# One decode step, attention beside a gated MLP: `w_out` as five rows on 128 lanes and seven rows on 32 lanes, all on SyncE's queue

## The chip, the cores and the metric

The kernel runs on one core of a Trainium2 chip. The metric is the device time of one execution in microseconds (us), from launch to the output in memory; smaller is better. Three runs of the kernel before took 662.22, 662.36 and 663.16 us, so the median is 662.36.

## The reference

For four tokens (batch 4, one position each, D = 640) the kernel adds a residual, an attention branch over a long cache and a gated MLP. Cut to what matters:

```python
xn = layernorm(x)                                   # x: 4 x 1 x 640, bf16
# A: 32 heads of 128, a cache of 4096 positions per head and batch element
q = (xn @ wq).reshape(4, 1, 32, 128).transpose(0, 2, 1, 3)
p = softmax(einsum('bhqd,bhkd->bhqk', q, k_cache) * 128 ** -0.5)
A = einsum('bhqk,bhkd->bhqd', p, v_cache).transpose(0, 2, 1, 3).reshape(4, 1, 4096) @ wo
# B: w_in 640 x 1728, w_out 864 x 640, Fh = 864
z = gelu(einsum('bsd,df->bsf', xn, w_in))
z1, z2 = z[..., :Fh], layernorm(z[..., Fh:])
g = einsum('ts,bsf->btf', w_sp, z2) + b_sp[None, :, None]
B = einsum('bsf,fd->bsd', z1 * g, w_out)
out = x + A + B
```

Each of the two caches is 134.2 MB; `w_out` is 1.1 MB of 282.2 MB read in all.

## The kernel before

**Attention.** The work is cut into 16 units, one for each group of eight heads and batch element (`NU` = 16). A unit's keys are 8.4 MB, held as 128 partitions by four pieces of 16 KB. The ring `k_ring` has seven places for such pieces; the values of a unit fill the one buffer `v_all`. For each piece, DVE multiplies keys by the query row (L514, 4.4 us), folds the halves (L520, 2.3 us), PE sums over the remaining 64 columns with an identity (L529), and DVE reduces (L542). PE then weighs the values (L599).

**Order of the loads.** All large loads are issued by SyncE (SP) on one DMA queue, in the order of the list `loads`. `pump()` issues the next entry as soon as the program has passed the last use of its places; the instruction itself then waits on semaphores. The list starts with half of unit 0's keys, then `load_w`, then the other half, then unit 1's keys. The first load of all, `wq`, is issued ahead of the list. `wq` and `w_in` lie in `v_all`, so the first values can be loaded only when the gated MLP has read its weights (the load at L157). Unit 2's keys wait for the first piece of unit 1 (the load at L146 that starts at 76.58 us).

**The gated MLP.** `gmlp()` is a generator whose steps are laid between the first key pieces. It multiplies `w_in` by the normalised tokens (L380, into `zT`), goes through GELU and the layer norm in a chain of small DVE steps (L390 to L474) with two PE matmuls of its own (L409, L456), and multiplies by `w_out` (L480), adding to `out_ps`.

**How `w_out` lies.** Its 864 rows are 6 x 128 + 96. The first 768 rows stand as six rows per partition: five of them (6,400 bytes a partition) in `v_all`, loaded at L120, and the sixth (1,280 bytes a partition) in `p_m`, loaded at L121. `p_m` is the buffer of the masked weights, which is not written before unit 0's softmax ends. The last 96 rows stand as four rows on each of 24 partitions, also in `p_m`, loaded by ScalarE's (ACT's) queue in five transfers of 5, 5, 5, 5 and 4 lanes (L115); a transfer takes every fifth lane. That makes `NFC` = 10 terms, six of 128 lanes and four of 24.

**The end.** The last values come in pieces, then `wo` for the last head group in six transfers (L210, L213); PE multiplies, ACT copies, and the result goes out in two transfers.

Of the kernel before, what the change touches and what calls it, by code (L numbers as in the profile page):

```python
# [10 lines left out]
BF16 = mybir.dt.bfloat16  # L11
ACT = mybir.ActivationFunctionType
ALU = mybir.AluOpType
# [4 lines left out]
def kernel(  # L18
# [14 lines left out]
    nc = tc.nc  # L33
    P = nc.NUM_PARTITIONS
    Bsz, Sq, D = A_x.shape
# [3 lines left out]
    Fh = F // 2  # L39
# [7 lines left out]
    QD = 32  # L47
    NQ = P // QD
    HT = 8
# [9 lines left out]
    RW = 8  # L59
    QW = HC * Dh  # L60
    RING = 2 * NK - 1
    NFF = Fh // P
    FR = 4
    FT = (Fh - NFF * P) // FR
    NFC = NFF + FR
    LS = 5
    NOH = D // 2
    CB = 4
    NG = NR // CB
# [8 lines left out]
    const = ctx.enter_context(tc.tile_pool(name="const", bufs=1))  # L78
    work = ctx.enter_context(tc.tile_pool(name="work", bufs=1))
    small = ctx.enter_context(tc.tile_pool(name="small", bufs=2))  # L80
    once = ctx.enter_context(tc.tile_pool(name="once", bufs=1))
    PSUM = bass.MemoryType.PSUM
    ps_s = ctx.enter_context(tc.tile_pool(name="ps_s", bufs=2, space=PSUM))
    ps_pv = ctx.enter_context(tc.tile_pool(name="ps_pv", bufs=2, space=PSUM))
# [3 lines left out]

    pad.tile([P, 96], FP32, name="pad")

    p_m = const.tile([P, 2, NG, CB, HT], BF16, name="p_m")
    x_bf = const.tile([Bsz, D], BF16)
    nc.scalar.dma_start(out=x_bf[:], in_=A_x.flatten_outer_dims())

# [6 lines left out]
    w_in_sb = v_all[:, DC * HD : DC * (HD + F)].rearrange("p (c n) -> p c n", c=DC)  # L101


    NV = NFF - 1
    at_v = -(-DC * (HD + F) // 256) * 256
    w_out_sb = v_all[:, at_v : at_v + NV * D].rearrange("p (k n) -> p k n", k=NV)
    p_w = p_m[:].rearrange("p n g c h -> p (n g c h)")
    at_p = -(-D // 256) * 256
    w_row_sb = p_w[:, 0:D]
    w_end_sb = p_w[:, at_p : at_p + FR * D].rearrange("p (r n) -> p r n", r=FR)  # L110
    nc.sync.dma_start(out=wq_sb, in_=A_wq.rearrange("(p c) n -> p c n", c=DC))

    w_end_rows = B_w_out[NFF * P : Fh].rearrange("(p r) n -> p r n", r=FR)
    for l in range(LS):
        nc.scalar.dma_start(out=w_end_sb[l:FT:LS], in_=w_end_rows[l:FT:LS])  # L115

    def load_w():
        nc.sync.dma_start(out=w_in_sb, in_=B_w_in.rearrange("(p c) n -> p c n", c=DC))
        w_rows = B_w_out[0 : NFF * P].rearrange("(p k) n -> p k n", k=NFF)
        nc.sync.dma_start(out=w_out_sb, in_=w_rows[:, 0:NV])  # L120
        nc.sync.dma_start(out=w_row_sb, in_=w_rows[:, NV])  # L121

    def run_of(cache, u):
        hg, b = divmod(u, Bsz)
# [49 lines left out]
    def wo_load(hg):  # L174
        return (lambda: load_wo(hg)), [WO_AT]

    loads = [k_load(0, 0, 2), (load_w, []), k_load(0, 2, 4), k_load(1)]
    for u in range(NU - 4):
        loads += [v_load(u), k_load(u + 2)]
        if u % Bsz == Bsz - 1:  # L180
# [188 lines left out]
    gm["ac"] = work.tile([1, 2 * Bsz], FP32, name="ac")  # L369
    gm["yT"] = work.tile([P, NFC, Bsz], BF16, name="yT")  # L370

    def gmlp():
        zz, gw, gt, gz = (gm[n] for n in ("zz", "gw", "gt", "gz"))
        zT = ps_pv.tile([P, 2, NFC, Bsz], FP32, tag="pv", name="zT")
        for t in range(2):
            f1 = t * Fh + NFF * P
            w_t = w_in_sb[:, :, t * Fh : f1].rearrange("p c (f k) -> p c k f", k=NFF)
            for k in range(NFC):
                for c in range(DC):
                    nc.tensor.matmul(  # L380
                        out=zT[: P if k < NFF else FT, t, k, :],
                        lhsT=w_t[:, c, k, :]
                        if k < NFF
                        else w_in_sb[:, c, f1 + k - NFF : f1 + FT * FR : FR],
                        rhs=xnT[:, c, 0:Bsz],
                        start=(c == 0),
                        stop=(c == DC - 1),
                    )
        yield
        nc.vector.tensor_copy(out=zz[:, :, 0:NFF, :], in_=zT[:, :, 0:NFF, :])  # L390
        nc.vector.tensor_copy(out=zz[:FT, :, NFF:], in_=zT[:FT, :, NFF:])
        nc.vector.tensor_tensor(out=gw[:], in0=zz[:], in1=zz[:], op=ALU.mult)
        nc.vector.tensor_scalar(
            out=gw[:], in0=gw[:], scalar1=0.044715, scalar2=1.0, op0=ALU.mult, op1=ALU.add
        )
        nc.vector.tensor_tensor(out=gw[:], in0=gw[:], in1=zz[:], op=ALU.mult)
        nc.scalar.activation(
            out=gt[:], in_=gw[:], func=ACT.Tanh, scale=math.sqrt(2.0 / math.pi)
        )
        yield  # L400
        nc.vector.tensor_scalar(
            out=gt[:], in0=gt[:], scalar1=1.0, scalar2=0.5, op0=ALU.add, op1=ALU.mult
        )
        nc.vector.tensor_tensor(out=gz[:, 0:2], in0=zz[:], in1=gt[:], op=ALU.mult)
        sq = gz[:, 2, :, :]
        nc.vector.tensor_tensor(out=sq, in0=gz[:, 1, :, :], in1=gz[:, 1, :, :], op=ALU.mult)

        s_ps = ps_m.tile([1, 2, NFC, Bsz], FP32, tag="m", name="ln_ps")
        nc.tensor.matmul(  # L409
            out=s_ps[:], lhsT=ones_sq[:, 0:1], rhs=gz[:, 1:3], start=True, stop=True  # L410
        )
        yield
        st, ac = gm["st"], gm["ac"]
        mean_t = st[:, 0:Bsz]
        ex2_t = st[:, Bsz : 2 * Bsz]
        var_t = st[:, 2 * Bsz : 3 * Bsz]
        rst_t = st[:, 3 * Bsz : 4 * Bsz]
        tmp_t = st[:, 4 * Bsz : 5 * Bsz]
        nc.vector.tensor_reduce(
            out=st[:, 0 : 2 * Bsz].rearrange("o (s b) -> o s b", s=2),  # L420
            in_=s_ps[:].rearrange("o s k b -> o s b k"),
            axis=AX.X,
            op=ALU.add,
        )
        nc.vector.tensor_scalar(
            out=st[:, 0 : 2 * Bsz],
            in0=st[:, 0 : 2 * Bsz],
            scalar1=1.0 / float(Fh),
            scalar2=None,
            op0=ALU.mult,  # L430
        )
        nc.vector.tensor_tensor(out=tmp_t, in0=mean_t, in1=mean_t, op=ALU.mult)
        nc.vector.tensor_tensor(out=var_t, in0=ex2_t, in1=tmp_t, op=ALU.subtract)
        nc.scalar.activation(
            out=rst_t, in_=var_t, func=ACT.Sqrt, bias=eps_tile[:1], scale=1.0
        )
        wsp_t = work.tile([1, 1], FP32, name="wsp_t")
        nc.vector.tensor_copy(out=wsp_t[:], in_=wsp_bf[:])
        bsp_t = work.tile([1, 1], FP32, name="bsp_t")
        nc.vector.tensor_copy(out=bsp_t[:], in_=bsp_bf[:])  # L440
        yield
        nc.vector.reciprocal(out=rst_t, in_=rst_t)
        nc.vector.tensor_scalar(
            out=ac[:, 0:Bsz], in0=rst_t, scalar1=wsp_t[:, 0:1], scalar2=None, op0=ALU.mult
        )
        nc.vector.tensor_tensor(out=tmp_t, in0=ac[:, 0:Bsz], in1=mean_t, op=ALU.mult)
        nc.vector.tensor_scalar(
            out=ac[:, Bsz : 2 * Bsz],
            in0=tmp_t,
            scalar1=-1.0,  # L450
            scalar2=bsp_t[:, 0:1],
            op0=ALU.mult,
            op1=ALU.add,
        )
        ac_ps = ps_m.tile([P, 2 * Bsz], FP32, tag="m", name="ac_ps")
        nc.tensor.matmul(  # L456
            out=ac_ps[:], lhsT=ones_sq[0:1, :], rhs=ac[:], start=True, stop=True
        )
        ac_sb = work.tile([P, 2 * Bsz], FP32, name="ac_sb")
        nc.scalar.copy(out=ac_sb[:], in_=ac_ps[:])  # L460
        yield
        nc.vector.tensor_tensor(
            out=sq,
            in0=gz[:, 1, :, :],
            in1=ac_sb[:, None, 0:Bsz].to_broadcast([P, NFC, Bsz]),
            op=ALU.mult,
        )
        nc.vector.tensor_tensor(
            out=sq,
            in0=sq,  # L470
            in1=ac_sb[:, None, Bsz : 2 * Bsz].to_broadcast([P, NFC, Bsz]),
            op=ALU.add,
        )
        nc.vector.tensor_tensor(out=gm["yT"][:], in0=gz[:, 0, :, :], in1=sq, op=ALU.mult)  # L474
        w_terms = [w_out_sb[:, k] for k in range(NV)] + [w_row_sb]
        w_terms += [w_end_sb[:FT, r] for r in range(FR)]
        for k in range(NFC):
            w = P if k < NFF else FT
            for half in range(2):
                nc.tensor.matmul(  # L480
                    out=out_sum(half),
                    lhsT=gm["yT"][:w, k, :],
                    rhs=w_terms[k][:, half * NOH : (half + 1) * NOH],
                    start=False,
                    stop=False,
                )
        yield
# [150 lines left out]
    def group_turn(hg):  # L638
# [2 lines left out]


        o_q = gr.pop(hg)[:].rearrange("p (q j) -> p q j", j=JR)
        o_n = once.tile([P, JR, PAR, QH], BF16, name="o_n")
        for e in range(PAR):
            nc.vector.scalar_tensor_tensor(  # L646
                out=o_n[:, :, e, :].rearrange("p j q -> p q j"),
# [3 lines left out]
                op0=ALU.mult,  # L651
                op1=ALU.mult,
            )
        o_t = once.tile([P, JR, QD], BF16, name="o_t")
        nc.vector.transpose(
            out=o_t[:].rearrange("p j q -> p (j q)"),
            in_=o_n[:].rearrange("p j e q -> p (j e q)"),
        )
        o_s = once.tile([P, JR, Bsz], BF16, name="o_s")
        nc.vector.tensor_tensor(  # L660
            out=o_s[:], in0=o_t[:, :, 0:Bsz], in1=o_t[:, :, Bsz : 2 * Bsz], op=ALU.add
        )
        gr[hg] = [o_s[:, j, :] for j in range(JR)]

# [160 lines left out]
```

## Time and profile before

| | us |
|---|---|
| median of three runs | 662.36 |
| runs | 662.22 to 663.16 |
| span of the profiled execution, first to last instruction | 660.5 |
| median less that span | 1.9 |
| DVE busy | 524.9 (79%) |
| PE busy | 310.9 (47%) |
| ACT busy | 29.8 (5%) |
| read from memory | 282.24 MB, 427 GB/s over the span |

Of the profiled execution only the span is recorded, no device time of its own. The page gives each engine's busy time, 40 slices of the span with the busy share of each engine in tenths, the DMA queues, and a chain of waits followed back from the last instruction. A time in the trace counts from the start of the span. The trace also holds the start and length of each DMA packet; q1 is SP's queue, q10 is ACT's, q8 and q14 carry instructions.

### The profile page before, as it was taken

The page shows a single profiled execution, that of the slowest core. Times are in us where ns is not written, and L with a number is a line of the kernel's source. Part 1 is how long each engine was busy: PE and PEld are TensorE (multiplying, and loading weights), DVE is VectorE, ACT ScalarE, POOL GpSimd, SP SyncE. Part 2 cuts the span into 40 slices and gives each one's busy share as a digit, 9 for nine tenths or more (in the row PEclk, how much of TensorE's full clock was granted, in tenths as well). Part 3 has the DMA queues.
Part 4 walks back from the last instruction along what each step waited for, and adds up shares of the span by engine and source line. Part 5 has one row for each costly group of instructions (what it writes and reads, how often), then busy time and mean ns, then how long its engine had stood idle before and what let it go on. Part 6 is the DMA issues. An engine that isn't in the chain of part 4 may idle for free.

```text
span 660.5 us, 4704 instructions
## 1 busy us (share of the span) xinstructions
PE 310.9 (47%) x2035; PEld 135.7 (21%) x2035; DVE 524.9 (79%) x332; ACT 29.8 (5%) x73; POOL 2.7 (0%) x12
## 2 busy tenths in 40 slices
PE   0274363526527362472536336362462633736366
PEld 0131122212203121130212112121130221212124
DVE  2578988959598795969959598695969969999950
ACT  0020000000000000000000000000000000000000
POOL 1000000000000000000000000000000000000000
PEclk9756686766768677576767768677576767678765
DMA  9999999999999999999999999999999999999997
GB/s 372 435 448 429 430 441 437 438 425 437 430 433 438 433 433 438 433 434 425 437 437 438 421 433 438 441 438 433 429 426 441 430 433 445 411 428 437 457 400 281
DMA packets 8113, 282.56 MB, mean 428 GB/s; under 512 B 888, under 2 KB 2180, under 8 KB 2588
## 3 DMA queue, kind: packets, MB, share of 16 engines
q1 hardware_dynamic: 8024, 282.12, 99.0%
q8 instruction: 16, 0.26, 0.1%
q10 hardware_dynamic: 68, 0.13, 0.1%
q14 instruction: 5, 0.04, 0.0%
HBM read 282.24 MB, written 0.01 MB: 427 GB/s over the span
## 4 chain that ended last, share of the span: by engine, by line
DMA 60%; DVE 30%; PE 9%; issue 1%; ACT 0%; DVEq 0%; SPq 0%
DMA k_ring<-in_A_k_cache_dram 52%; DVE k_ring L514 15%; DVE k_ring L520 8%; PE s_ps L529 7%; DMA v_all<-in_A_v_cache_dram 4%; DMA k_ring<-in_A_wo_dram 3%; DVE s_sb L542 2%; DVE p_m L575 1%; DVE m L551 1%; PE out_ps L668 1%; DVE o_n L646 1%; PE zT L380 1%; PE pv L599 1%; DVE mt L553 0%; PE out_ps L480 0%
## 5 line engine op out<-in xcount | busy, mean ns | idle before, releaser
L514 DVE TENSOR_TENSOR k_ring<-k_ring,qbc 128x8192 bf16<-128x8192 bf16 x64 | 282.7, 4418 | 86.3 <-DMA k_ring<-in_A_k_cache_dram 86.3
L529 PE MATMUL s_ps<-k_ring,ident 128*128 128x512 bf16 x512 | 201.1, 564 | 313.7 <-DVE k_ring L520 313.5
L529 PEld LDWEIGHTS <-ident 128*128 128x128 bf16 x512 | 65.4, 129 | 427.7 <-issue 383.7
L520 DVE TENSOR_TENSOR k_ring<-k_ring 128x4096 bf16<-128x4096 bf16 x64 | 145.9, 2279 | 0.0
L599 PE MATMUL pv<-v_all,p_m 128*32 128x512 bf16 x960 | 60.2, 407 | 0.0
L542 DVE TENSOR_REDUCE s_sb<-s_ps 128x64 f32<-128x512 f32 x64 | 43.6, 682 | 5.7 <-PE s_ps L529 5.7
L575 DVE TENSOR_TENSOR p_m<-p_c,own 128x2048 bf16<-128x2048 bf16 x16 | 36.5, 2284 | 0.7 <-ACT p_c L564 0.7
L599 PEld LDWEIGHTS <-p_m 128*32 128x32 bf16 x992 | 25.8, 103 | 39.4 <-issue 17.1
L564 ACT ACTIVATE p_c<-s_sb,nm 128x256 bf16<-128x256 f32 x16 | 8.1, 508 | 331.2 <-DVE nm L558 331.2
L630 PEld LDWEIGHTS o_ps<-o_rows,pick 128*128 128x128 f32 x96 | 19.5, 280 | 4.1 <-issue 3.0
L630 PE MATMUL o_ps<-o_rows,pick 128*128 128x128 f32 x96 | 18.6, 357 | 0.0
L611 ACT COPY o_rows<-pv 128x512 f32<-128x512 f32 x16 | 9.4, 586 | 167.4 <-PE pv L599 167.4
L293 DVE TENSOR_SCALAR q_rows<-q_ps 128x512 bf16<-128x512 f32 x2 | 1.4, 692 | 12.3 <-PE q_ps L285 12.3
L786 DVE TENSOR_TENSOR o_n_last<-o_last,rden_all 128x32 bf16<-128x32 f32 x1 | 0.2, 192 | 12.3 <-PE o_last L778 12.3
L504 ACT CAST qbc<-qbc_ps 128x128 bf16<-128x128 f32 x16 | 4.3, 266 | 101.7 <-PE qbc_ps L496 101.7
L285 PE MATMUL q_ps<-v_all,xnT 128*32 128x512 bf16 x40 | 4.3, 618 | 8.9 <-DMA v_all<-in_A_wq_dram 8.9
L551 DVE TENSOR_REDUCE m<-s_sb 128x1 f32<-128x256 f32 x16 | 6.7, 420 | 0.6
L496 PE MATMUL qbc_ps<-q_rows,of_row 128*128 128x128 bf16 x32 | 6.0, 277 | 0.6 <-DVE q_rows L293 0.6
L496 PEld LDWEIGHTS <-of_row 128*128 128x128 bf16 x32 | 4.2, 134 | 8.3 <-issue 7.8
L668 PE MATMUL out_ps<-k_ring,o_s 128*4 128x320 bf16 x48 | 4.4, 331 | 2.2 <-DVE o_s L660 2.2
L685 PE MATMUL o_last<-hot,o_rows 128*128 128x8 f32 x32 | 4.9, 280 | 0.7 <-ACT o_rows L611 0.7
L685 PEld LDWEIGHTS o_last<-hot,o_rows 128*128 128x128 f32 x32 | 4.8, 225 | 1.8 <-ACT o_rows L611 1.6
(89 smaller groups left out, 74.6 us busy)
## 6 DMA issues: line engine op xcount, KB each, us to landing
k_ring<-in_A_k_cache_dram SPq DMA_DIRECT2D x6, 4096.0 KB, 24.8
v_all<-in_A_v_cache_dram SPq DMA_DIRECT2D x2, 4096.0 KB, 28.8
v_all<-in_A_wq_dram SPq DMA_DIRECT2D x1, 5120.0 KB
k_ring<-in_A_v_cache_dram SPq DMA_DIRECT2D x1, 4096.0 KB
k_ring<-in_A_wo_dram SPq DMA_DIRECT2D x3, 1280.0 KB, 20.1
v_all<-in_B_w_in_dram SPq DMA_DIRECT2D x1, 2160.0 KB
k_ring<-in_A_v_cache_dram SPq DMA_DIRECT2D x1, 2048.0 KB
k_ring<-in_A_v_cache_dram SPq DMA_DIRECT2D x1, 1024.0 KB
```

Source lines behind the costliest of these rows:

```text
L496: nc.tensor.matmul(out=qb_ps[:], lhsT=of_row[:, e, b].rearrange("p k f l -> p (k f l)"), rhs=q_rows[e][:, hg, :], start=(e == 0), stop=(e ...
L514: nc.vector.tensor_tensor(out=t, in0=t, in1=qbcs[u][:, None, :].to_broadcast([P, HC, Dh]), op=ALU.mult)
L520: nc.vector.tensor_tensor(out=t[:, :, 0:HD2], in0=t[:, :, 0:HD2], in1=t[:, :, HD2:Dh], op=ALU.add)
L529: nc.tensor.matmul(out=s[:], lhsT=ident[:], rhs=t[:, :, g * RW : (g + 1) * RW], start=(g == 0), stop=(g == m - 1),)
L542: nc.vector.tensor_reduce(out=scores[u][:, r * HC : (r + 1) * HC], in_=sums_ps.pop(n)[:], axis=AX.X, op=ALU.add,)
L551: nc.vector.tensor_reduce(out=m1[:], in_=scores[u][:], axis=AX.X, op=ALU.max)
L575: nc.vector.tensor_tensor(out=p_m[:, u % 2], in0=p_c.pop(u)[:].rearrange("p (g c) -> p g c", c=CB)[:, :, :, None].to_broadcast([P, NG, CB, HT]
L599: nc.tensor.matmul(out=pvs[u][cg * QD : (cg + 1) * QD, :], lhsT=p_m[:, u % 2, g0 + n].rearrange("p c h -> p (c h)"), rhs=v_at[:, n * CB : ...
L611: nc.scalar.copy(out=o[:].rearrange("p c d -> p (c d)"), in_=pvs.pop(u)[:])
L630: nc.tensor.matmul(out=gr[hg][:], lhsT=pick[:, c, Bsz - 1 - b : P + Bsz - 1 - b], rhs=o[:, c, :], start=(b == 0 and c == 0), stop=(b == Bs ...
L668: nc.tensor.matmul(out=out_sum(half), lhsT=o, rhs=wo_sb[:, n, half * NOH : (half + 1) * NOH], start=False, stop=(hg == HG - 1 and n == HT ...
L685: nc.tensor.matmul(out=o_last[0][:, :, :, u % Bsz], lhsT=o[:, c, :], rhs=hot[:, c, :].rearrange("p (k e) -> p k e", e=PAR), start=(c == 0) ...
```

## The change

`w_out` is laid out anew. The first 640 rows stand as five rows per partition in `v_all` (one transfer, 6,400 bytes a partition). The other 224 rows stand as seven rows on each of 32 partitions, in the buffer that `p_m` occupies, loaded by four transfers of eight lanes (8,960 bytes a lane, every fourth lane). These four are issued by SP, behind the first half of unit 0's keys and ahead of `w_in`. ACT issues none of `w_out`. The terms number 12 instead of 10: five of 128 lanes and seven of 32. The buffer grows so that the seven rows fit (4,480 elements), and the small tiles `o_n`, `o_t` and `o_s` of `group_turn` move from a pool of their own into its end.

```diff
-    NFF = Fh // P
-    FR = 4
-    FT = (Fh - NFF * P) // FR
-    NFC = NFF + FR
-    LS = 5
+    FA, FL, LS = 5, 32, 4
+    FB = (Fh - FA * P) // FL
+    NFC = FA + FB
...
-    p_m = const.tile([P, 2, NG, CB, HT], BF16, name="p_m")
+    p_buf = const.tile(
+        [P, max(2 * NR * HT + JR * (2 * QD + Bsz), FB * D)], BF16, name="p_m"
+    )
+    p_end = p_buf[:, 2 * NR * HT :]
+    p_m = p_buf[:, 0 : 2 * NR * HT].rearrange("p (n g c h) -> p n g c h", n=2, g=NG, c=CB)
...
-    w_end_rows = B_w_out[NFF * P : Fh].rearrange("(p r) n -> p r n", r=FR)
-    for l in range(LS):
-        nc.scalar.dma_start(out=w_end_sb[l:FT:LS], in_=w_end_rows[l:FT:LS])
+    w_b_rows = B_w_out[FA * P : Fh].rearrange("(p k) n -> p k n", k=FB)
+
+    def load_w_b():
+        for l in range(LS):
+            nc.sync.dma_start(out=w_b_sb[l:FL:LS], in_=w_b_rows[l:FL:LS])
 
     def load_w():
         nc.sync.dma_start(out=w_in_sb, in_=B_w_in.rearrange("(p c) n -> p c n", c=DC))
-        w_rows = B_w_out[0 : NFF * P].rearrange("(p k) n -> p k n", k=NFF)
-        nc.sync.dma_start(out=w_out_sb, in_=w_rows[:, 0:NV])
-        nc.sync.dma_start(out=w_row_sb, in_=w_rows[:, NV])
+        nc.sync.dma_start(
+            out=w_a_sb, in_=B_w_out[0 : FA * P].rearrange("(p k) n -> p k n", k=FA)
+        )
...
-    loads = [k_load(0, 0, 2), (load_w, []), k_load(0, 2, 4), k_load(1)]
+    loads = [k_load(0, 0, 2), (load_w_b, []), (load_w, []), k_load(0, 2, 4), k_load(1)]
...
-        o_n = once.tile([P, JR, PAR, QH], BF16, name="o_n")
+        o_n = p_end[:, 0 : JR * QD].rearrange("p (j e q) -> p j e q", j=JR, e=PAR)
```

The matmul loops of `gmlp()` and the copies of `zT` follow the new lanes; the copies, the GELU and the layer norm handle 96 columns instead of 80 (12 terms by 4 tokens by 2 halves).

More of the change, by code (lines that the diff above doesn't have):

```diff
@@ L61 @@
     RING = 2 * NK - 1
-    NFF = Fh // P
-    FR = 4
-    FT = (Fh - NFF * P) // FR
-    NFC = NFF + FR
-    LS = 5
+    FA, FL, LS = 5, 32, 4
+    FB = (Fh - FA * P) // FL
+    assert FA * P + FB * FL == Fh
+    NFC = FA + FB
     NOH = D // 2
@@ L80 @@
     small = ctx.enter_context(tc.tile_pool(name="small", bufs=2))
-    once = ctx.enter_context(tc.tile_pool(name="once", bufs=1))
     PSUM = bass.MemoryType.PSUM
@@ L101 @@
     w_in_sb = v_all[:, DC * HD : DC * (HD + F)].rearrange("p (c n) -> p c n", c=DC)
-    NV = NFF - 1
     at_v = -(-DC * (HD + F) // 256) * 256
[L106 to L110, printed above, removed]
+    w_a_sb = v_all[:, at_v : at_v + FA * D].rearrange("p (k n) -> p k n", k=FA)
+    w_b_sb = p_buf[0:FL, 0 : FB * D].rearrange("p (k n) -> p k n", k=FB)
     nc.sync.dma_start(out=wq_sb, in_=A_wq.rearrange("(p c) n -> p c n", c=DC))
-    w_end_rows = B_w_out[NFF * P : Fh].rearrange("(p r) n -> p r n", r=FR)
-    for l in range(LS):
-        nc.scalar.dma_start(out=w_end_sb[l:FT:LS], in_=w_end_rows[l:FT:LS])
+    w_b_rows = B_w_out[FA * P : Fh].rearrange("(p k) n -> p k n", k=FB)
+    def load_w_b():
+        for l in range(LS):
+            nc.sync.dma_start(out=w_b_sb[l:FL:LS], in_=w_b_rows[l:FL:LS])
     def load_w():
         nc.sync.dma_start(out=w_in_sb, in_=B_w_in.rearrange("(p c) n -> p c n", c=DC))
-        w_rows = B_w_out[0 : NFF * P].rearrange("(p k) n -> p k n", k=NFF)
-        nc.sync.dma_start(out=w_out_sb, in_=w_rows[:, 0:NV])
-        nc.sync.dma_start(out=w_row_sb, in_=w_rows[:, NV])
+        nc.sync.dma_start(
+            out=w_a_sb, in_=B_w_out[0 : FA * P].rearrange("(p k) n -> p k n", k=FA)
+        )
     def run_of(cache, u):
@@ L370, with lanes @@
     gm["yT"] = work.tile([P, NFC, Bsz], BF16, name="yT")
+    def lanes(k):
+        return P if k < FA else FL
     def gmlp():
@@ L375, in gmlp @@
         for t in range(2):
-            f1 = t * Fh + NFF * P
-            w_t = w_in_sb[:, :, t * Fh : f1].rearrange("p c (f k) -> p c k f", k=NFF)
+            w_t = w_in_sb[:, :, t * Fh : (t + 1) * Fh]
             for k in range(NFC):
+                w_k = (
+                    w_t[:, :, k : FA * P : FA]
+                    if k < FA
+                    else w_t[:, :, FA * P + k - FA : Fh : FB]
+                )
                 for c in range(DC):
                     nc.tensor.matmul(
[L381 to L384, printed above, removed]
+                        out=zT[0 : lanes(k), t, k, :],
+                        lhsT=w_k[:, c],
                         rhs=xnT[:, c, 0:Bsz],
@@ L389, in gmlp @@
         yield
-        nc.vector.tensor_copy(out=zz[:, :, 0:NFF, :], in_=zT[:, :, 0:NFF, :])
-        nc.vector.tensor_copy(out=zz[:FT, :, NFF:], in_=zT[:FT, :, NFF:])
+        nc.vector.tensor_copy(out=zz[:, :, 0:FA, :], in_=zT[:, :, 0:FA, :])
+        nc.vector.tensor_copy(out=zz[:FL, :, FA:], in_=zT[:FL, :, FA:])
         nc.vector.tensor_tensor(out=gw[:], in0=zz[:], in1=zz[:], op=ALU.mult)
@@ L474, in gmlp @@
         nc.vector.tensor_tensor(out=gm["yT"][:], in0=gz[:, 0, :, :], in1=sq, op=ALU.mult)
-        w_terms = [w_out_sb[:, k] for k in range(NV)] + [w_row_sb]
-        w_terms += [w_end_sb[:FT, r] for r in range(FR)]
+        w_terms = [w_a_sb[:, k] for k in range(FA)] + [w_b_sb[:, r] for r in range(FB)]
         for k in range(NFC):
-            w = P if k < NFF else FT
             for half in range(2):
@@ L481, in gmlp @@
                     out=out_sum(half),
-                    lhsT=gm["yT"][:w, k, :],
+                    lhsT=gm["yT"][0 : lanes(k), k, :],
                     rhs=w_terms[k][:, half * NOH : (half + 1) * NOH],
@@ L653, in group_turn @@
             )
-        o_t = once.tile([P, JR, QD], BF16, name="o_t")
+        o_t = p_end[:, JR * QD : 2 * JR * QD].rearrange("p (j q) -> p j q", j=JR)
         nc.vector.transpose(
-            out=o_t[:].rearrange("p j q -> p (j q)"),
-            in_=o_n[:].rearrange("p j e q -> p (j e q)"),
+            out=p_end[:, JR * QD : 2 * JR * QD], in_=p_end[:, 0 : JR * QD]
         )
-        o_s = once.tile([P, JR, Bsz], BF16, name="o_s")
+        o_s = p_end[:, 2 * JR * QD : JR * (2 * QD + Bsz)].rearrange("p (j b) -> p j b", b=Bsz)
         nc.vector.tensor_tensor(
-            out=o_s[:], in0=o_t[:, :, 0:Bsz], in1=o_t[:, :, Bsz : 2 * Bsz], op=ALU.add
+            out=o_s, in0=o_t[:, :, 0:Bsz], in1=o_t[:, :, Bsz : 2 * Bsz], op=ALU.add
         )
```

## The prediction

> **What bounds the kernel now.** I read the page's DMA lines first, then the DMA share by stretch, then the chain of waits, and last the packet records. The page:
>
> ```profile
> DMA  9999999999999999999999999999999999999997
> q1 hardware_dynamic: 8024, 282.12, 99.0%
> q8 instruction: 16, 0.26, 0.1%
> q10 hardware_dynamic: 68, 0.13, 0.1%
> ```
>
> The 16 DMA engines are busy in every slice, nearly all with SP's queue (q1). By stretches (last two columns: DMA share, GB/s):
>
> ```profile
> 2.00:100.00 98.00, 43.60 (x306) 19.04 (x307) 67.50 (x63) 8.14 (x14) 1.23 (x6) 0.70 1.00 430
> 500.00:600.00 100.00, 47.25 (x256) 19.44 (x256) 92.84 (x57) 3.77 (x11) 0.00 (x0) 0.70 1.00 431
> 653.00:657.00 4.00, 2.83 (x38) 1.46 (x37) 0.19 (x1) 0.00 (x0) 0.00 (x0) 0.50 0.67 238
> ```
>
> The share is 1.00 from 2 us on and falls only in the last four: in the packet records no engine idles between 3 and 653 us, and then the engines finish one after another, from 653.2 to 656.9 us. So the end is set by the DMA engine with the most work, not by the mean (about 655.7). The chain of waits shows the part around the change:
>
> ```profile
> 36.70 4.03 PE zT L380 x100
> ...
> 55.39 2.92 PE out_ps L480 x20
> 58.31 3.42 PE s_ps L529 x8
> ...
> 72.98 3.57 PE s_ps L529 x8
> ...
> 76.58 25.24 DMA k_ring<-in_A_k_cache_dram
> ```
>
> This chain is followed through whatever released an issue; that unit 2's keys were issued at 76.58 us does not mean that the DMA engines waited for them. The timeline of SP gives the issues:
>
> ```profile
> 16.62 20.23 SPq L146 DMA_DIRECT2D k_ring<-in_A_k_cache_dram  x2
> 56.92 0.33 SPq L157 DMA_DIRECT2D v_all<-in_A_v_cache_dram  x1
> 76.58 0.33 SPq L146 DMA_DIRECT2D k_ring<-in_A_k_cache_dram  x1
> ```
>
> Set against the packets: the values issued at 56.92 have their first packet at 60.85 us on the engine furthest ahead, the keys issued at 76.58 at 80.17. An issue needs about 1.0 us to its first packet (`wq`: issued 0.74, first packet 1.74), so the cover is 2.9 and 2.6 us on the leading engine, and 2.8 us more on the last one.
>
> **The DMA work, engine by engine.** From one packet's start to the next on the same engine, 1,280 bytes take 0.050 us, 5,120 take 0.193, 8,192 take 0.305 and 10,240 take 0.381. 8,960 bytes lie between the last two: 0.333 us (estimate). Between transfers I see 0.006 us more.
>
> Removed on all engines: the sixth row, 8 packets, 0.40 us. Removed on five engines: the ACT transfers, one packet per lane; following the packets engine by engine, four engines carry five of them (0.97 us) and one carries four (0.77). Added: four transfers of eight lanes. Five lanes used five engines, the same each time, so I take eight lanes as eight engines, the same each time: 4 x 0.333 + 4 x 0.006 = 1.36 us on each. If the eight include the five, the sums are: four engines 1.36 - 0.40 - 0.97 = -0.01; one +0.19; three +0.96; the other eight -0.40. If the eight are others, five engines gain 1.2 to 1.4 us and eight lose 0.96: the worst case is the same +0.96. The total over 16 engines falls by 0.6 engine-us, 0.04 a piece: the change balances bytes differently and saves none.
>
> The Trainium skill ("DMA: Bandwidth & Descriptors", "Why a DMA increments its semaphore by 16 and not by 1") says that such a transfer takes the largest number of engines up to 16 that divides the outer counts of both sides, and the lowest-numbered ones. By that rule the eight include the five and three engines gain 0.96 us; the trace agrees as far as it goes (five lanes, five engines, the same each time). The same page's advice against confining a transfer to few engines speaks against both layouts.
>
> **Who is last.** At 645 us, nine engines have 285 to 308 KB left and seven have 212 to 258. The nine are the eight that also fetch PE's instructions (16 packets of 16,384 bytes on q8, each stalling one engine by 0.87 to 1.01 us, about 41 us apart, in rotation) and the one with four narrow packets. Working off the remaining packets at the steps above, and adding the fetch at 648 us, the ends come out as 656.9 (an engine with five narrow packets), 656.8, 656.7 (two), 656.6, 656.4, and three about 656.0, one of which meets a further fetch at 654.9 and so ends near 656.8; the packets really end at 656.86. Of these nine, three carry narrow packets now and stay within +0.19; six do not, and three of the eleven engines without narrow packets gain 0.96. If none of the three is among the six, the end stays (chance 10/165, all choices alike); otherwise it moves to 656.7 + 0.96 at most for those without a late fetch, +0.1 to +0.8.
>
> The fetches move as well: 24 more matmuls with 24 weight loads are 48 instructions on PE, at 3,814 before and 16 fetches some 0.2 of a pitch, so the last fetch comes some 7 us earlier, near 647. It then costs its engine the full 0.9 us ahead of the tail. If that engine is also one of the three, it ends near 656.0 + 0.96 + 0.9 = 657.8, +0.95. I take +0.55, between nothing and +0.95, nearer the latter because most choices of the three hit a late engine.
>
> **The compute around it.** PE: 20 more matmuls at L380, 4.03/100 = 0.04 us each, +0.81 on the chain before the GELU. Four more at L480, 2.92/20 = 0.146 each, +0.58, behind the ten that read `v_all`. DVE: 11 small steps of about 0.2 us on 96 instead of 80 columns: 0 to +0.45, I take +0.2. So the values are issued 1.0 us later (57.9) and unit 2's keys 1.6 (78.2); their packets can start at 58.9 and 79.2. The leading engine, if among those that lose 0.40 us, needs them at 60.45 and 79.77. Covered by 1.5 and 0.6 us; price nothing. Were the cover gone, only leading engines would idle, and these finish 2 us early anyway. After that DVE waits for keys in every unit (it starts at 101.92 us on a landing), so the delay is absorbed.
>
> SP: four issues more and two fewer, 0.33 us each, in a stretch with packets queued. The semaphores are reused in another order: in the changed program `w_in` waits for `wq` to land, the five rows for the first half keys, the second half keys for `w_sp`, unit 1's keys for `b_sp`. `wq` has landed by 16.45 (PE's first use), the queue then holds keys until 24.29; the keys land at 26.02, `w_in` lasts until 29.4; `w_sp` has its packet at 25.5 and is needed by 30. Price nothing; without cover, queued behind each wait are all further loads. ACT: five issues fewer (0.7 us each), so the layer norm of x comes some 3 us earlier, but PE then waits for `wq` until 16.45 regardless. First product: bound by the slowest engine's half keys (26.02), whose lateness comes from its first packet at 2.76 us, so not earlier. Moving `o_n`, `o_t`, `o_s`: same shapes, no new waits in the order; nothing.
>
> Sum: 660.5 + 0.55 = 661.05 of span. The profiled run's own device time is not recorded; the median lies 1.86 above the span, so 662.36 + 0.55 = 662.9. A measurement here tells about 0.2% (1.3 us) from no change, so I call this the same.
>
> **Rivals.** *Slower: the extra lanes fall on the engine that ends last.* For it: six of the nine late engines are free to be hit; the starting order differs by 1.0 us between engines (first packets 1.74 to 2.76), which another execution may deal to one of the three. Against: the leads of 0.2 to 0.9 us soak up part. Price: +0.96, with a fetch moved in front and a late start up to +0.96 + 0.9 = 1.86, so 663.7 to 664.2; it counts as slower once the engine hit stands within 0.5 us of the last with its fetch still to come. 0.20.
>
> *Slower: the lanes do not spread.* If eight lanes ran on four engines, these would carry eight packets more or less: 2.7 us in place of 0.97, 663.6 to 664.5; on one, 10.8 us, 672. Against: the five-lane transfers spread. 0.02.
>
> *Faster: narrow or small transfers cost more than their packets.* Six transfers go and four come. If the five engines' load on a second queue slowed the start, or each transfer had a cost of its own, up to the 1.2 us between the last engine and the mean could go, and a little more of the start: 661 or below. Against: successive transfers follow at 0.006 us. 0.08. [...]
>
> **How the numbers follow.** Forecast (same) 0.70, slower 0.20 + 0.02, faster 0.08. The forecast's own range is 0 to +0.95 about the median, with the 0.5 us by which the runs scatter: 661.8 to 663.6. The range takes in the slower rival and part of the faster: 661.6 to 664.3.
>
> **What would show it.** Right: DMA share 1.00 from 2 to 653 us; the last DMA packet 0 to 1 us later; PE zT near 4.8 us; unit 2's keys issued near 78 us with no gap in the DMA; a thinner spread between lanes early on. Wrong: a DMA share below 1.00 near 60 or 80 us (the cover failed), a first product clearly before 26 us followed by an earlier end (the start was worth more), or the span moving by over 1.3 us with the same packets on the last engine.

## The result, and the profile after

The changed kernel takes 663.43 us (median of 12 runs, 663.12 to 664.93) against 662.37 before (median of 12): +1.06 us. The ratio, which takes in all runs and not the medians alone, is 1.0018, with a 95% interval of 1.001 to 1.0026. The kernel is slower, then, by a little that is clear of the noise. The ratio is inside the 0.2% which the prediction called the same, on its slow side, and the median is inside its range of 661.6 to 664.3. The profiled execution took 663.12 us with a span of 661.3.

The page after, the parts that answer to those of before:

```profile
DMA  9999999999999999999999999999999999999996
...
q1 hardware_dynamic: 7944, 282.25, 99.0%
q8 instruction: 16, 0.26, 0.1%
...
q10 hardware_dynamic: 20, 0.01, 0.0%
```

ACT's queue (q10) is nearly empty: the narrow rows have moved to q1, and fewer, larger packets carry the same bytes. The DMA engines are still the bound. The same stretches:

```profile
653.00:657.00 4.00, 2.69 (x44) 1.45 (x42) 0.19 (x1) 0.00 (x0) 0.00 (x0) 0.50 0.77 279
...
2.00:100.00 98.00, 44.24 (x324) 19.87 (x325) 67.79 (x63) 7.47 (x14) 1.24 (x6) 0.70 0.99 425
```

In the last stretch the share is 0.77 instead of 0.67: the work of the last engines reaches further out. In the first it is 0.99 and 425 GB/s instead of 1.00 and 430: something is missing early on. The last packet ends at 657.56 us, 0.70 later than before. The chain of waits and SP's issues show where the early part went:

```profile
36.47 5.99 PE zT L387 x120
...
57.31 3.45 PE out_ps L483 x24
60.76 3.54 PE s_ps L532 x8
...
75.55 3.57 PE s_ps L532 x8
...
79.16 22.94 DMA k_ring<-in_A_k_cache_dram
```

```profile
58.84 0.33 SPq L157 DMA_DIRECT2D v_all<-in_A_v_cache_dram  x1
79.16 0.33 SPq L146 DMA_DIRECT2D k_ring<-in_A_k_cache_dram  x1
```

The 120 small matmuls of `zT` take 5.99 us, not the 4.84 that the prediction had; the first values are issued 1.92 us later than before (predicted 1.0) and unit 2's keys 2.58 later (predicted 1.6). And the cover does not hold. From 57 to 66 us, the kernel before and then the changed one (DMA share and GB/s last):

```profile
57.00:66.00 9.00, 6.02 (x22) 2.05 (x21) 6.92 (x4) 0.00 (x0) 0.00 (x0) 0.69 0.99 430
```

```profile
57.00:66.00 9.00, 6.98 (x32) 2.38 (x33) 6.23 (x5) 0.00 (x0) 0.00 (x0) 0.50 0.94 380
```

These shares count a packet whole in the stretch in which it starts, so they are rough over 9 us. The packet records tell it more exactly. They name no engine; which packets belong to one engine is read from one packet's end meeting the next one's start. Three engines run dry, at 60.42, 60.59 and 60.84 us, and the first packets of the values that they can get come at 61.55, 61.62 and 61.88 us, 2.7 to 3.0 us after the issue. Together that is 3.2 us of idle time; before, there was none.

The engines that do not run dry lose time too. The first packet of the values (65,536 bytes) takes 2.42 us on all sixteen engines before, and 2.60 to 3.76 us on all sixteen in the changed kernel, 8.0 us more in all. Idle time and longer packets together make 0.7 us per engine.

So two theories stand. *Balance*: three more DMA engines carry narrow packets, and the last one ends later. *Stall*: the values come late, engines lose time waiting, and that moves the end. The experiments separate them. They were run in three groups, each on one chip beside the kernel before. The median of the kernel before was 662.34 us in the first group (e1 to e4), 662.35 in the second (e5 to e8) and 662.45 in the third (e9 and e10), so medians of different groups are compared to about 0.1 us.

### The profile page after: what moved, and what is told of

The parts are those of the page before. It is cut to its first block, busy times and chain, and to the rows that moved or that the text cites. A ratio compares the mean times of both kernels' runs of the same rounds, so it can differ in the third digit from the quotient of the medians.

```text
span 661.3 us, 4750 instructions
## 1 busy us (share of the span) xinstructions
PE 311.4 (47%) x2059; PEld 135.3 (20%) x2059; DVE 525.3 (79%) x332; ACT 29.8 (5%) x73; POOL 2.7 (0%) x12
## 4 chain that ended last, share of the span: by engine, by line
DMA 59%; DVE 30%; PE 10%; issue 1%; ACT 0%; SPq 0%; DVEq 0%
DMA k_ring<-in_A_k_cache_dram 52%; DVE k_ring L517 15%; DVE k_ring L523 8%; PE s_ps L532 7%; DMA v_all<-in_A_v_cache_dram 4%; DMA k_ring<-in_A_wo_dram 3%; DVE s_sb L545 2%; DVE p_m L578 1%; DVE m L554 1%; PE zT L387 1%; PE out_ps L670 1%; DVE p_m L649 1%; PE pv L602 1%; PE out_ps L483 1%; DVE mt L556 0%
## 5 line engine op out<-in xcount | busy, mean ns | idle before, releaser
L633 PEld LDWEIGHTS o_ps<-o_rows,pick 128*128 128x128 f32 x96 | 17.4, 253 | 3.9 <-issue 3.1
L633 PE MATMUL o_ps<-o_rows,pick 128*128 128x128 f32 x96 | 16.2, 325 | 0.0
L387 PE MATMUL zT<-xnT,v_all 128*32 128x4 bf16 (+1 forms) x120 | 6.2, 188 | 0.0
L387 PEld LDWEIGHTS <-v_all 128*32 128x32 bf16 (+1 forms) x120 | 6.2, 142 | 0.0
L670 PE MATMUL out_ps<-k_ring,p_m 128*4 128x320 bf16 x48 | 4.4, 331 | 2.3 <-DVE p_m L662 2.3
```

The lines of the kernel that those rows point to most:

```text
L387: nc.tensor.matmul(out=zT[0 : lanes(k), t, k, :], lhsT=w_k[:, c], rhs=xnT[:, c, 0:Bsz], start=(c == 0), stop=(c == DC - 1),)
L633: nc.tensor.matmul(out=gr[hg][:], lhsT=pick[:, c, Bsz - 1 - b : P + Bsz - 1 - b], rhs=o[:, c, :], start=(b == 0 and c == 0), stop=(b == Bs ...
L670: nc.tensor.matmul(out=out_sum(half), lhsT=o, rhs=wo_sb[:, n, half * NOH : (half + 1) * NOH], start=False, stop=(hg == HG - 1 and n == HT ...
```

## The experiments

**e1_again.** No edit.

> The changed kernel itself, once more beside the others on one chip. Two theories are tested with the four runs. Balance: the seven-row lanes give three more DMA engines 0.96 us of work, and the last engine ends later by 0.5 to 0.95 us whatever the compute does. Stall: the chain of the gated MLP got 1.9 us longer (PE zT 5.99 us for 120 matmuls against 4.03 for 100), the first values were issued at 58.84 us instead of 56.92, leading DMA engines idled for up to 1.5 us at 60 to 61 us, and some of them are last at the end, because each later loses twice 0.9 us to instruction fetches. Both expect here about 1.0 us over the kernel before (663.1 to 663.7).

Measured: 663.42 us (663.02 to 664.84), ratio 1.0019, interval 1.001 to 1.0027. The result repeats, and so does its scatter: the kernel before stays within 0.7 us, this one spreads over 1.8. In its profile the values are issued at 58.55 us. Engines idle for 5.1 us in all, and the values' first packets take 6.4 us more than before: 0.7 us per engine again.

**e2_contiguous_columns.**

```diff
-                    else w_t[:, :, FA * P + k - FA : Fh : FB]
+                    else w_t[:, :, FA * P + (k - FA) * FL : FA * P + (k - FA + 1) * FL]
```

> The changed kernel with one edit: the seven narrow terms take 32 neighbouring columns of w_in each, instead of every seventh column. The number of matmuls, all loads and all bytes stay; the terms meet the wrong columns, so that part of the MLP computes something else. If the pace of the narrow weight loads (54 ns from one to the next in the changed kernel, 25 ns before) comes from the step between columns (7 against 4 elements), PE zT falls from 6.0 to about 3.7 us, the first values are issued near 56.6 us, and no DMA engine idles at 60 us. Stall theory: the time falls back to that of the kernel before, within 0.3 us (662.1 to 662.7). Balance theory: it stays at +0.5 to +1.0 us. If the pace comes from the 32 lanes and not from the step, zT stays near 6 us and nothing changes.

Measured: 662.97 us (662.65 to 663.24), ratio 1.0009, interval 1.0 to 1.0018, which just touches 1. The trace:

```profile
36.22 3.94 PE zT L387 x120
```

```profile
57.00:66.00 9.00, 6.02 (x23) 2.04 (x20) 6.26 (x4) 0.00 (x0) 0.00 (x0) 0.50 1.02 439
```

The step between the columns of the narrow terms is what made `zT` long: 120 matmuls now take 3.94 us, less than the 4.03 of the 100 before. The values are issued at 56.54 us and no engine idles from 57 to 66. The time falls by 0.45 us against e1 and the scatter to 0.6, but 0.6 us remain over the kernel before. Each theory had half of it.

**e3_longer_chain**, on the kernel before.

```diff
-            for k in range(NFC):
+            for k in [0, 1, 2, 3] + list(range(NFC)):
```

> The kernel before with one edit: four of its six-lane-step terms are computed twice in each half of zT (40 more matmuls of 128 lanes, at 47 ns each 1.9 us), the same numbers and the same loads. The first values should be issued near 58.8 us, as in the changed kernel. Stall theory: slower by 0.5 to 1.0 us (662.9 to 663.4), with an idle stretch of the DMA near 60 us. Balance theory: no change within 0.2 us (662.2 to 662.6).

Measured: 663.25 us, but from 662.32 to 665.33; ratio 1.0016, interval 1.0006 to 1.0025. Three of 11 runs are as fast as the kernel before, three are above 664. The trace is of a run at 662.74:

```profile
36.84 5.90 PE zT L380 x140
```

```profile
57.00:66.00 9.00, 6.44 (x28) 2.12 (x29) 6.77 (x5) 0.00 (x0) 0.00 (x0) 0.50 0.94 395
```

With the loads and the layout of before, 1.9 us more on the chain (values issued at 58.92 us) make the time slower and uncertain. In this profiled run, 0.4 us slower than the median before, engines idle for only 0.8 us in all and the values' first packets take 3.0 us more, 0.2 us per engine. At this delay the cover is just used up: in some runs nothing is lost, in others up to 3 us. The stall theory is right that values issued late make the kernel slower, and the median lies in its range; the steady loss that it expected is not there.

**e4_loads_alone.** The loads of the changed kernel under the matmuls of before.

```diff
-        nc.scalar.dma_start(out=w_end_sb[l:FT:LS], in_=w_end_rows[l:FT:LS])
+            nc.sync.dma_start(out=w_b_sb[l:FL:LW], in_=w_b_rows[l:FL:LW])
...
-        nc.sync.dma_start(out=w_out_sb, in_=w_rows[:, 0:NV])
-        nc.sync.dma_start(out=w_row_sb, in_=w_rows[:, NV])
+            out=w_a_sb, in_=B_w_out[0 : FA * P].rearrange("(p k) n -> p k n", k=FA)
```

> The loads of the changed kernel (five rows on 128 lanes, seven rows on 32 lanes in four transfers of eight, all on SyncE) under the matmuls of the kernel before (six terms of 128 lanes, four of 24), which then multiply by other rows than they should. The small tiles lie as in the changed kernel; the lanes that are not loaded are set to zero by GpSimd at the start. Balance theory: slower by 0.5 to 0.95 us (662.9 to 663.3) with the first values issued near 57 us and no idle DMA. Stall theory: no change within 0.3 us (662.1 to 662.7).

Measured: 662.83 us (662.73 to 663.0), ratio 1.0007, interval 0.9998 to 1.0016. The interval includes 1, but all 11 runs lie above the median of before, within 0.27 us of one another. `zT` takes 4.03 us again, the values are issued at 56.57 us, and no engine idles:

```profile
57.00:66.00 9.00, 6.02 (x21) 2.04 (x18) 6.80 (x4) 0.00 (x0) 0.00 (x0) 0.69 1.01 437
```

The last packet ends at 657.24 us against 656.86. So by the medians the loads alone cost 0.49 us, steadily, and the longer chain is left for the rest with its scatter, as e2 and e3 have it.

**e5_sixteen_lanes.**

```diff
-    FA, FL, LS = 5, 32, 4
+    FA, FL, LS = 5, 32, 2
```

> The changed kernel with the seven rows loaded by two transfers of sixteen lanes instead of four of eight; compute unchanged. If a transfer of sixteen lanes runs on sixteen engines, each engine carries two packets of 8,960 bytes (0.68 us) instead of four on eight engines (1.36 us) and none on the others, so the last engine should gain up to 0.68 us. What the late first values cost (issue at 58.8 us, engines idle near 61 us) stays. Balance theory alone: 662.5 to 662.9. Both theories together, as the four runs so far suggest (loads alone +0.5 us, longer chain alone +0.9 us): 662.8 to 663.2, with the wide scatter of the changed kernel. If the lanes do not spread over sixteen engines: no better than the changed kernel, 663.4.

Measured: 664.91 us (663.82 to 665.62, 5 runs), ratio 1.0038, interval 1.0026 to 1.005: slower, against all expectations. The packet records show a reason why the lanes gain little. Four transfers of eight lanes make 32 packets of 0.338 us each. In two transfers of sixteen, the same 32 packets take 0.338 to 0.644 us, on average 0.449 (e6 has 0.338 to 0.656, on average 0.447). The work is spread, but there is a third more of it. That sixteen engines get in each other's way when they write to the same 32 partitions fits this and was not tested by itself. The Trainium skill ("SBUF — State Buffer", "Door 1: The DMA port swizzle") says that partitions 0 to 31 reach 8 of 16 ports; by that rule sixteen engines would share eight ports, and the longer packets agree. The start also got later: the first half keys were complete on their last engine at 26.29 us (25.47 in the changed kernel), the first values were issued at 59.49, and the engine served last got unit 2's first packet 2.2 us after it had run dry. Which of these weighs how much was not separated.

**e6_sixteen_lanes_contiguous.** Both edits, of e5 and e2.

> The same with two transfers of sixteen lanes and, in addition, neighbouring columns of w_in for the narrow terms (which then are the wrong columns). Both costs are taken away: the first values issued near 56.6 us, the packets even over the engines. Both theories together: 662.0 to 662.5, at or below the kernel before, with little scatter. If only the queue's order or the four waits of SyncE behind other landings had cost the time, it would stay near 663.

Measured: 663.19 us (662.91 to 663.77), ratio 1.0014, interval 1.0005 to 1.0022. That is above the range expected and 0.2 us above e2, so sixteen lanes do not repair the balance; with `zT` short (3.99 us), 1.7 us of e5's loss are gone. The first values were issued at 57.81 us, later than in e2, because the first product started at 27.09 instead of 25.64.

**e7_chain_twice_as_long**, on the kernel before.

```diff
-            for k in range(NFC):
+            for k in [0, 1, 2, 3] * 2 + list(range(NFC)):
```

> The kernel before with eight terms of zT computed twice in each half (80 more matmuls, 3.8 us), loads unchanged, so the first values are issued near 60.8 us. In the run with 1.9 us more, idle engines got their first packet of the values 2.2 to 3.6 us after the issue. Stall theory: now nearly all engines wait for the values, until 63 to 64.5 us, and unit 2's keys, issued near 80.6 us, are late too; slower by 1.5 to 2.5 us (663.8 to 664.8), with a median clearly above that of the shorter delay. If the idle stretch cost only engines that finish early anyway: +0.9 us or less, as with the shorter delay.

Measured: 664.52 us (663.95 to 665.15, 6 runs), ratio 1.0032, interval 1.002 to 1.0044: +2.2 us, as the stall theory had it.

```profile
37.36 7.78 PE zT L380 x180
```

```profile
57.00:66.00 9.00, 6.21 (x28) 2.12 (x29) 7.00 (x5) 1.35 (x2) 0.00 (x0) 0.53 0.91 359
```

The first product started late, at 26.90 us, so the values were issued only at 61.32. Now 13 engines run out of keys between 60.75 and 61.87 us, and the values' first packets come at 62.28 to 63.64. Engines idle for 16.9 us in all, and the first packets (2.75 to 3.50 us each) add 11.6: 1.8 us per engine. In this run (664.78 us) the last packet of the loads ends at 659.37 us, 2.5 later than before.

**e8_one_row_on_96.** Six rows on 128 lanes and one row on each of 96.

```diff
-    FR = 4
+    FR = 1
...
-    for l in range(LS):
-        nc.scalar.dma_start(out=w_end_sb[l:FT:LS], in_=w_end_rows[l:FT:LS])
...
+        nc.sync.dma_start(out=w_end_sb[0:FT], in_=w_end_rows)
```

> A version of its own: six rows on 128 lanes as in the kernel before, and the other 96 rows as one row on each of 96 lanes, in one transfer on SyncE behind the sixth row. That makes 7 terms, the narrow one over neighbouring columns of w_in: 70 matmuls in zT (about 3.1 us instead of 4.0) and 14 at the output (2.1 us instead of 2.9). If 96 lanes spread over sixteen engines, each carries six packets of 1,280 bytes (0.3 us) instead of 0.97 us on five: the five gain 0.67 us, the others lose 0.3. Both theories together: 661.8 to 662.3, faster than the kernel before by up to 0.5 us and no wider in scatter. If the last engine is not one of the five in most runs: no change or +0.3 us.

Measured: median 662.41 us, ratio 1.0023, interval 1.0004 to 1.0043 (the five high runs raise it). Seven of 12 runs lie at 662.27 to 662.42, the other five at 663.2 to 668.5. In the usual run it equals the kernel before; the profile (662.41 us) shows the values issued at 55.45 us and no idle engine. What lifts those five is open, since no trace of one is kept. It is no better kernel.

**e9_lanes_twice**, on e4.

```diff
+    w_2_sb = p_buf[FL : 2 * FL, 0 : FB * D].rearrange("p (k n) -> p k n", k=FB)
+    for l in range(LW):
+        nc.scalar.dma_start(out=w_2_sb[l:FL:LW], in_=w_b_rows[l:FL:LW])
```

> The run with the changed loads under the old matmuls (0.5 us slower than the kernel before), with one edit: ScalarE's queue loads the same seven rows a second time, in four more transfers of eight lanes, into partitions 32 to 63. If eight lanes always mean the same eight DMA engines, each of these carries another 1.36 us. Balance theory: the end moves by about that much more, 1.2 to 1.4 us over the run with single loads (663.9 to 664.3), with the first values issued near 56.6 us and no engine idle at 61 us. If the 0.5 us came from anything else (the order of the queue, the waits of SyncE on other landings, where the small tiles lie): no more than 0.3 us on top (662.7 to 663.1).

Measured: 664.18 us (663.84 to 664.35), ratio 1.0024, interval 1.0015 to 1.0034. The median is 1.35 us above that of e4; each against the kernel before of its own group, the step is 1.73 - 0.49 = 1.24. The packets make 1.36. The values are issued at 57.46 us and no engine idles from 57 to 66 us, so no stall is in it.

**e10_no_narrow_loads**, on e4.

```diff
-    loads = [k_load(0, 0, 2), (load_w_b, []), (load_w, []), k_load(0, 2, 4), k_load(1)]
+    loads = [k_load(0, 0, 2), (load_w, []), k_load(0, 2, 4), k_load(1)]
```

> The same base without any load of the seven rows: 287 KB are not read, and the terms multiply by zeros that GpSimd writes at the start. It shows how much any layout of these rows could gain. Balance theory: against the kernel before, engines without narrow packets lose 0.40 us (the sixth row) and the five others 1.2 to 1.4 us; the last engine is as often one as the other, so the end comes 0.4 to 0.6 us earlier than before (661.8 to 662.0), and 0.9 to 1.1 us earlier than with the seven rows on eight engines. If balance plays no part and only the bytes count: 287 KB of 282 MB, 0.1%, 0.66 us less than the run with the changed loads (662.2). SyncE then waits for no landing before the second half keys, which in two earlier versions went with slow outliers.

Measured: 661.48 us (661.35 to 661.73), ratio 0.9985, interval 0.9976 to 0.9994. The median is 1.35 us below that of e4; each against the kernel before of its own group, the step is 0.97 + 0.49 = 1.46. The two queue lines of e9 and e10 show how little is moved for these 2.7 us:

```profile
q1 hardware_dynamic: 7944, 282.25, 98.8%
...
q10 hardware_dynamic: 84, 0.29, 0.1%
```

```profile
q1 hardware_dynamic: 7880, 281.96, 99.1%
...
q10 hardware_dynamic: 20, 0.01, 0.0%
```

Evenly over 16 engines, each load of 0.287 MB would cost 0.66 us at 27.1 GB/s an engine (65,536 bytes in 2.418 us). It costs about 1.35, because it runs on eight. And the kernel before, with narrow packets on five engines and the sixth row on all, stands 1.0 us above the same base.

## Why the prediction was right or wrong

**The DMA bound and the last engine: right.** The forecast rested on the end being set by the engine with most work. None, one and two loads on eight engines give 661.48, 662.83 and 664.18 us: 1.35 us a step, or 1.46 and 1.24 when each is set against the kernel before of its own group, against 4 x 0.334 + 4 x 0.006 = 1.36 from start to start of the packets as measured (0.333 estimated). That the steps count nearly in full says that the last engine of the base is one of the eight, or level with one. The expectation for e10 had taken it as often outside them, and so came out 0.3 us too high.

**The size from the loads: right, in part by luck.** +0.55 us was forecast, between 0 and 0.95; the loads alone measure +0.49. The range came from counting the work that each engine had left, with the instruction fetches on top; the value was chosen inside it, so that it hit to 0.06 us is luck. The part about the fetches did not come true: the last two start at 648.3 and 655.9 us in the changed kernel, not some 7 us earlier than before (647.9 and 654.9). And one sum is off, though nothing hangs on it: by the prediction's own terms (4 x -0.01, 0.19, 3 x 0.96, 8 x -0.40) the total over 16 engines falls by 0.17 engine-us, not 0.6.

**The compute around it: wrong.** The step said "Covered by 1.5 and 0.6 us; price nothing". The sign that the prediction had named for this, a DMA share below 1.00 near 60 us, is in the trace (0.94). The step failed in three places.
- The pace of PE. "0.04 us each" was the mean of two kinds. From one weight load to the next the trace before has 47 ns for 128 columns that are 6 elements apart and 25 ns for 24 columns 4 apart; the changed kernel has 39 ns for 128 columns 5 apart and 54 ns for 32 columns 7 apart; e2 has 25 ns for 32 neighbouring columns. The sum 50 x 39 + 70 x 54 is 5.7 us, near the 5.99 measured; the added 0.81 us was in truth 1.96. That one mean does not serve for a new layout could have been seen from the two values of before.
- The latency of an issue. "About 1.0 us to its first packet" is the first engine's. The row it was taken from (`wq`, issued at 0.74 us) has the first packet on its sixteenth engine at 2.76, 2.0 us after the issue. The values' first packets came 1.0 to 2.3 us after the issue in e7, on the engines that had run dry 2.7 to 3.0 us after it in the changed kernel, and on one in e3 3.9. The delay that the prediction forecast left 2.5 us between the issue (57.9) and the first engine's need (60.45); the trace left 1.6 (58.84 and 60.42). In e10, 3.4 us were enough for no engine to idle. The "2.8 us more on the last one" is misread too: its first packets come at 62.67 and 82.07 us, 1.8 and 1.9 us behind the two times named.
- Who pays. "Were the cover gone, only leading engines would idle, and these finish 2 us early anyway." e7 refutes it: late values cost 2.2 us at the end. In the changed kernel all sixteen engines lost time to longer first packets, those that are last at the end among them. The lost time per engine goes with the loss at the end: 0.0 us in the kernel before and in e4, 0.2 in e3's profiled run, 0.7 in the changed kernel, 1.8 in e7, and those last three runs are slower than the kernel before by 0.4, 0.75 (0.49 of it from the loads) and 2.4 us. From 100 to 650 us the engines idle for 1.1 to 1.2 us in all in every run, so nothing later makes the difference. Why the packets lengthen is open, and no run separates them from the idle time.

**The sum.** 0.49 us from the loads, and from the chain the 0.57 that is then left, make the 1.06; e2, with the chain's pace restored, takes 0.45 of these back. The forecast had the first term and missed the second. The measured 1.06 us lies above the 0.95 that the forecast allowed for the loads; the 663.43 us are inside its own 661.8 to 663.6 only through the 0.5 us added for scatter, and that is luck.

**The rivals.** The slower rival, the extra lanes on the engine that ends last, is what the loads do, at half its price. That the lanes do not spread is refuted by e9. That narrow transfers have a cost of their own beyond their packets, the faster rival, is not borne out by the steps of 1.24 to 1.46 us: packets and boundaries explain 1.36.

## What to carry to other kernels

Where the DMA engines are full from start to end, count bytes per engine, not per kernel: a load on eight engines costs twice its share. Cover for a late issue is to be measured on the engine that is served last, and the price is not paid by leading engines alone: look at how long the packets take that follow the issue. When a matmul's weights are read with a step, look up the pace at that step and number of columns, not the mean of the group.

## What the runs showed of the hardware

With bf16 weights and 4 moving columns, 32 weight columns took 54 ns from one load to the next at a step of 7 elements and 25 at a step of 1 (the changed kernel and e2, which differ in this step alone); 24 columns at a step of 4 also took 25. The granted clock did not matter: e5 has the 54 ns in its part at 1.00 and in its part at 0.50. The number of columns does: in e8, 96 neighbouring columns took 45 ns. 128 columns took 39 ns at a step of 5 and 47 at 6; no run has them at a smaller step, so what the step costs there is open. The Trainium skill ("SBUF — State Buffer", "Door 1: The DMA port swizzle") gives 16-byte lines in SBUF and says that at least two hits per line are needed for full speed; by that rule a step of 4 (8 bytes) is free and 7 (14 bytes) is not, and the trace agrees. The same passage goes on to call up to 8 bf16 elements free, and there the 54 ns at 7 disagree.

Packets of 65,536 bytes took 2.42 us where the queue was never empty; the first ones of values that were issued 1.6 us before the first engine ran dry took 2.60 to 3.76.

Two transfers of sixteen lanes into 32 partitions made 32 packets cost 14.4 engine-us, four of eight lanes 10.8.
